# First batch's query and key rows loaded unit by unit, its pooled product given a bank of its own, and VectorE adding it before x is split

## The chip, the cores and the metric

The kernel runs on one core of a Trainium2 chip. The metric is the device time of one execution in microseconds (us), shown as the median of three runs. A core has TensorE (PE, with PEld for weight loads), VectorE (DVE), ScalarE (ACT), GpSimd (POOL) and SyncE (SP); SP issues the transfers, as does ACT where the code says `nc.scalar.dma_start`.

## The reference, cut to what matters

Attention over q, k, v of shape (8 batches, 8 heads, 576 rows, 64), then a feed-forward block with float32 weights of 512x2048 and 2048x512.

```python
q_d, k_d, v_d = (t.reshape(B, H, S // 4, 4, D).mean(axis=3) for t in (q, k, v))
out_d = sm_attn(q_d, k_d, v_d)                  # 144 pooled rows, full softmax
out_up = np.repeat(out_d, 4, axis=2)
mask = np.abs(pos[:, None] - pos[None, :]) < 4  # a band of 7 keys
out_local = softmax(where(mask, q @ k.T / 8, -1e9)) @ v
x = (out_up + out_local)                        # laid out as (4608, 512)
h = x @ w_in
out = (h * clip(h + 3, 0, 6) / 6) @ w_out
```

Each pooled output row is repeated four times and added to four rows of the banded (local) output.

## The kernel before, in words

**The two stages.** x has 4608 tokens, cut into nine chunks of 512. For each chunk TensorE runs 16 steps f of a first product (L977, 12 matmuls of 512 columns into bank `h`) and 16 of a second (L1027, 12 matmuls into four banks `o0` to `o3`). The products are made from parts: x and each weight block are split into a high and a low part (float32r), and three of the four cross products are taken. ScalarE and VectorE do the gate between the two products (L983, L987, L991, L995). The weights come as 32 blocks of 512 KB and are turned into their two parts once, during the first chunk: two ScalarE passes (L180, L192), a VectorE pass that joins bits (L185), a ScalarE cast (L198) and a subtraction (L202, on VectorE or GpSimd).

**The attention** goes by units: one unit is two heads of one batch, so a batch has four. The first batch (b = 0, `direct`) is special, because TensorE has nothing else to do until it is done. Its q and k are loaded for two units at a time (a duo): for the first duo in three transfers of 192 KB per tensor, for the second in one of 576 KB (L257). Partition p gets nine rows in a row, and TensorE turns these with 128x128 transposes, three to a bank (L270). An eviction (L122 on VectorE, L120 on ScalarE) writes the three results into `qkd` with a step of nine elements, so that the columns stand in the order of the tokens. Then come, for each unit:
- the sums of four columns of q and k (`pool4`: L351 on VectorE, L355 and L357 on GpSimd);
- the pooled scores (L451), their softmax (L507, L500, L528, L535 on 432 columns), the transposes of the weights (L544);
- the banded scores (L654 writes the mask, L662 the products), the greatest of each row (L507), the subtraction (L510), the exponent (L513), the total (L522), the reciprocal (L528), the division (L535 on 640 columns) and the transposes (L687);
- v in two forms: windows of 64 rows (L374, L378) for the banded product, and rows in fours (L385, L387) whose sums are made by GpSimd (L401, L402) and, for the last 16 pooled rows, by TensorE (L414).

**The end of a first-batch unit** is where the change lies. `pv_d` (L632) multiplies the pooled weights with the summed v. The right operand is read with a broadcast, each of 72 columns four times, so each matmul gives 288 columns straight into one of the two banks `x` of the unit, for two heads, two halves and two groups of rows. `pv` (L705) then adds the 20 banded products of 64x57 or 64x60 to the same columns, accumulating in PSUM. The split of x reads these banks: a high part (L122 or L120 CAST) and a low part (L881, VectorE only in the first chunk), and a copy takes the last 64 tokens of the batch, which belong to the next chunk, to `tail`. The second batch already works another way: its `pv_d` (L629) gives 144 columns into a bank `od`, ScalarE scales them, and VectorE adds the two (L713).

**What sets the order.** The program first plans all work as operations with engine, guessed cost, due time and the buffers that they take and free; a list planner then places them, engine by engine, and writes the instructions in that order. So every engine runs a fixed list. PE also gets matmuls of no use (`busy`, L1079) where the planner sees it waiting before the first product. `PEN` holds the planner's preferences between engines. A transfer waits for the one issued eight transfers before it, since there are eight completion semaphores.

**Lines after.** In the changed program most lines stand 4 to 16 lower in number: L977 becomes L972, L1027 L1022, L632 and L629 L620, L705 L691, L713 L696, L881 L875, L662 L648, L687 L673, L535 L530, L414 L409, L385 L380, L387 L382, L270 L318, L257 L311 and L313, L351 L346, L336 L295, L342 L301, L987 L982.

Of the kernel before, what the change touches and what calls it, by code (L numbers as in the profile page):

```python
# [19 lines left out]
P = 128  # L20
# [36 lines left out]
def tile_local_down_attention_moe(ctx, tc, q_all, k_all, v_all, _qk_loc, _v_loc, w_in, w_out, ident_d, _mask_d, out):  # L57
# [161 lines left out]
    xt, px = {}, {}  # L219
# [11 lines left out]
    def plan_duo(b, d, masked):  # L231
# [6 lines left out]
        qk, evicts, users = {}, {}, {"q": [], "k": []}  # L238
# [6 lines left out]
        if b < BY_PE:  # L245
            for kind, t in (("q", q_all), ("k", k_all)):
                evicts[kind] = []
                hk = kind, b, d
                rk = ("rawd", hk)
                raw = {}  # L250
                pieces_ = []
                step = 3 if d == 0 else 9
                for first in range(0, 9, step):
                    def ld(first=first, t=t, raw=raw, rk=rk, step=step):
                        if not raw:
                            raw["t"] = buf(rk[0], rk[1], [P, 9, ROW])
                        nc.sync.dma_start(  # L257
                            raw["t"][:, first:first + step],
                            src(t, row0 + first, [[9 * ROW, P], [ROW, step], [1, ROW]]))

                    pieces_.append(op("SP", 0.5, ld, take=[rk], size=dma(P, step * 512), dl=-1.0))
                    loads.append(pieces_[-1])
                for g in range(3):
                    st = {}
                    key = kind, b, d, g

                    def tr(g=g, st=st, key=key, raw=raw):
                        st["ps"] = ps = bank(PS, key)
                        for i in range(3):
                            nc.tensor.transpose(out=ps[:, i * P:(i + 1) * P], in_=raw["t"][:, 3 * g + i], identity=ident)  # L270

                    def ev(eng, g=g, st=st, key=key, kind=kind, hk=hk):
                        if kind not in qk:
                            qk[kind] = buf("qkd" + k0, hk, [P, 2, S])
                        dst = qk[kind].rearrange("e u (p t) -> e t (u p) ", t=9)[:, 3 * g:3 * g + 3]
                        copy_on(eng, dst, st["ps"][:, :3 * P].rearrange("e (t p) -> e t p", t=3))
# [12 lines left out]
        if b < BY_PE:  # L289
            for kind in "qk":  # L290
                plan.free_after(("qkd" + k0, (kind, b, d)), users[kind])
# [1262 lines left out]
```

## Time and profile before

| | us |
|---|---|
| median of three runs | 926.05 |
| lowest, highest of them | 921.72, 927.14 |
| the profiled execution | 926.6 |
| its span, first to last instruction | 924.7 |
| PE busy | 907.5 (98%) |
| DVE, ACT, POOL busy | 535.5, 438.1, 218.1 |
| mean granted TensorE clock | 0.994 |

The profile is one execution, so 1.9 us of its 926.6 lie outside the span. The lists of instructions in order of time show start and duration; durations of instructions that follow each other on an engine overlap a little, so a stretch is read from starts. "Windows" give the busy time of each engine in a stretch, with the clock that TensorE was granted. The chain of waits is the chain of work that ended last, followed back from the end: in it PE has 94%, and the two products of the feed-forward block 84%.

### The profile page before, as it was taken

What the parts mean: (1) busy time and instruction counts of PE and PEld (TensorE: products, weight loads), DVE (VectorE), ACT (ScalarE), POOL (GpSimd) and SP (SyncE); (2) the same over time, 40 slices, a digit from 0 to 9 for tenths busy, and PEclk for the clock granted to TensorE, in tenths of its full rate; (3) what the DMA queues carried; (4) which work ended last, traced back from release to release, by engine and by line L of the source; (5) the groups of instructions that cost most, each with busy time, mean ns of one, the idle gap of its engine ahead of it and who ended that gap; (6) DMA issues with size and microseconds to landing.
All of it is one profiled execution on the core that took longest, in us unless ns stands there. A gap on an engine that the chain in (4) does not pass through costs nothing.

```text
span 924.7 us, 19205 instructions
## 1 busy us (share of the span) xinstructions
PE 907.5 (98%) x7046; PEld 736.0 (80%) x7046; DVE 535.5 (58%) x968; ACT 438.1 (47%) x1437; POOL 218.1 (24%) x296
## 2 busy tenths in 40 slices
PE   7899999999999999999999999999999999999997
PEld 4577777888788888888888888888888888888886
DVE  7898677666675568456855576557644432233222
ACT  4788653755564456345545455445542222222221
POOL 4545611132252233023402240224201000000000
PEclk9899999999999999999999999999999999999999
DMA  8999343566665455445555556455532010001001
GB/s 211 311 218 288 68 113 62 117 133 127 116 140 108 100 108 126 103 95 114 110 130 104 102 113 133 76 101 113 132 76 54 1 46 1 1 1 46 0 1 46
DMA packets 311759, 93.49 MB, mean 101 GB/s; under 512 B 251377, under 2 KB 297841, under 8 KB 311665
## 3 DMA queue, kind: packets, MB, share of 16 engines
q1 hardware_dynamic: 311280, 91.69, 44.2%
q8 instruction: 55, 0.90, 0.4%
q10 hardware_dynamic: 384, 0.58, 0.2%
q14 instruction: 40, 0.32, 0.1%
HBM read 69.60 MB, written 22.61 MB: 100 GB/s over the span
## 4 chain that ended last, share of the span: by engine, by line
PE 94%; DMA 2%; DVE 1%; SPq 1%; POOL 1%; issue 0%; ACT 0%; ACTq 0%; DVEq 0%; POOLq 0%
PE h L977 42%; PE o L1027 42%; PE a L662 2%; PE h L705 1%; PE h L613 1%; PE a L468 1%; DMA arena<-in_v_dram 1%; PE o L632 1%; DMA pl<-arena 0%; PE a L705 0%; PE a L451 0%; SPq L257 0%; DMA early<-in_v_dram 0%; PE o L705 0%; PE h L468 0%
## 5 line engine op out<-in xcount | busy, mean ns | idle before, releaser
L1027 PE MATMUL o<-wp,rounded 128*128 128x512 f32 x1728 | 412.0, 392 | 0.0
L977 PE MATMUL h<-rounded,wp 128*128 128x512 f32 x1728 | 405.5, 390 | 2.5 <-DVE first L713 2.4
L977 PEld LDWEIGHTS h<-rounded,wp 128*128 128x128 f32 x1728 | 323.0, 188 | 71.7 <-issue 3.7
L1027 PEld LDWEIGHTS o<-wp,rounded 128*128 128x128 f32 x1728 | 321.5, 188 | 68.4 <-issue 0.8
L983 ACT ACTIVATE arena<-h 128x512 f32<-128x512 f32 x144 | 85.8, 596 | 197.5 <-PE h L977 195.3
L987 DVE SCALAR_TENSOR_TENSOR arena<-arena,h 128x512 f32<-128x512 f32 x144 | 98.1, 681 | 134.2 <-ACT arena L983 133.7
L995 DVE TENSOR_TENSOR rounded<-arena,rounded 128x512 fp32r<-128x512 f32 x115 | 81.0, 705 | 129.4 <-PE o L1027 107.0
L991 ACT CAST rounded<-arena 128x512 fp32r<-128x512 f32 x144 | 88.9, 618 | 109.9 <-PE o L1027 59.3
L518 ACT ACTIVATE arena<-arena 128x64 f32<-128x64 f32 x240 | 80.3, 337 | 0.2
L995 POOL TENSOR_TENSOR rounded<-arena,rounded 128x512 fp32r<-128x512 f32 x29 | 39.0, 1344 | 76.0 <-PE o L1027 40.3
L342 DVE STREAM_TRANSPOSE arena<-arena 128x576 f32<-128x576 f32 x56 | 42.8, 764 | 23.9 <-DMA arena<-in_k_dram 15.9
L535 POOL TENSOR_TENSOR arena<-arena 128x640 f32<-128x640 f32 (+1 forms) x22 | 24.9, 1133 | 130.8 <-DVE arena L528 130.8
L401 POOL TENSOR_TENSOR arena<-arena 32x256 f32<-32x256 f32 (+1 forms) x27 | 20.4, 754 | 119.9 <-DMA arena<-in_v_dram 119.1
L518 ACT ACTIVATION_READ_ACCUMULATOR arena<-arena 128x1 f32 x240 | 45.4, 189 | 0.0
L637 ACT ACTIVATE arena<-h 128x144 f32<-128x144 f32 x24 | 7.0, 291 | 67.5 <-PE h L613 67.5
L494 ACT ACTIVATE arena<-arena 128x1 f32<-128x1 f32 (+1 forms) x79 | 15.2, 193 | 42.1 <-DVE arena L507 42.1
L399 DVE TENSOR_REDUCE arena<-arena 128x128 f32<-128x512 f32 (+1 forms) x25 | 26.5, 1059 | 13.6 <-PE h L613 11.1
L580 DVE STREAM_TRANSPOSE arena<-arena 128x384 f32<-128x384 f32 (+1 forms) x48 | 22.2, 467 | 20.8 <-DMA arena<-pd 20.5
L357 POOL TENSOR_TENSOR arena<-arena 128x144 f32<-128x144 f32 x54 | 31.1, 576 | 4.2
L402 POOL TENSOR_TENSOR arena<-arena 32x128 f32<-32x128 f32 (+1 forms) x27 | 12.2, 452 | 74.8 <-PE h L613 62.8
L599 DVE STREAM_TRANSPOSE arena<-arena 128x640 f32<-128x640 f32 x24 | 20.2, 844 | 14.2 <-DMA arena<-pl 14.1
L662 PE MATMUL a<-arena 64*64 64x64 f32 x1160 | 28.2, 222 | 0.0
(190 smaller groups left out, 798.9 us busy)
## 6 DMA issues: line engine op xcount, KB each, us to landing
rawp<-in_w_in_dram SPq DMA_DIRECT2D x16, 512.0 KB
rawp<-in_w_out_dram SPq DMA_DIRECT2D x16, 512.0 KB
arena<-in_q_dram SPq DMA_DIRECT2D x112, 72.0 KB
arena<-in_k_dram SPq DMA_DIRECT2D x112, 72.0 KB
pl<-arena SPq DMA_DIRECT2D x24, 320.0 KB
arena<-pl SPq DMA_DIRECT2D x96, 80.0 KB
arena<-in_v_dram SPq DMA_DIRECT2D x28, 256.0 KB
out_dram<-arena SPq DMA_DIRECT2D x89, 72.0 KB
```

The lines of the kernel that those rows point to most:

```text
L342: nc.vector.transpose(out=qk[kind], in_=qk[kind])
L357: eng.tensor_tensor(t, t, x[:, :, r], op=ALU.add)
L399: eng.tensor_reduce(out=vd, in_=raw.rearrange("p r e -> p e r"), op=ALU.add, axis=AX.X)
L518: nc.scalar.activation(x[:, j], x[:, j], AF.Exp, bias=m[:, j:j + 1], scale=0.125, accum_out=s[:, j:j + 1])
L535: eng.tensor_tensor(x, x, s.unsqueeze(2).broadcast_to(list(x.shape)), op=ALU.mult)
L662: nc.tensor.matmul(st["ps", g][half:half + WIN, jj * D:jj * D + WIN], qk_of("q")[hs, k_first:k_first + WIN], qk_of("k")[hs, k_first:k_firs ...
L977: nc.tensor.matmul(st["ps"], win[f][:, wt, kk * P:(kk + 1) * P], xs[part][:, kk], start=(kk == 0 and i == 0), stop=(kk == NK - 1 and i == ...
L983: nc.scalar.activation(st["t"], st["ps"], AF.Relu, bias=3.0)
L987: nc.vector.scalar_tensor_tensor(out=t, in0=t, scalar=6.0, in1=st["ps"], op0=ALU.min, op1=ALU.mult)
L991: nc.scalar.copy(st["gh"], st["t"])
L995: eng.tensor_tensor(st["gl"], st["t"], st["gh"].bitcast(F32), op=ALU.subtract)
L1027: nc.tensor.matmul(otile[n, m], gt[:, ms], wout[f][:, wt], start=(f == 0 and i == 0), stop=(f == NF - 1 and i == 2),)
```

## The change

What it does, for the first batch alone but for one planner preference:

- q and k are loaded for each unit by itself: 512 rows as 128 partitions of four rows (256 KB, one 2 KB piece per partition) and the other 64 rows of q and k as the two halves of a ninth tile (32 KB each). So there are 16 transfers where there were 8. Those of k are issued by ScalarE, those of q by SyncE.
- A unit has nine transposes as before, in banks of four, four and one. The evictions write `qkd` in order of memory and read PSUM with a step of 128 elements instead.
- `pv_d` of the first batch gives 144 columns into its own bank, half as many matmuls of half the columns; a copy brings them to `od` in SBUF. `pv` starts its own accumulation.
- VectorE adds `od`, each column four times, to the banded product (L696): 288 and 224 columns into a new SBUF buffer `x0`, and 64 into `tail`, instead of the copy.
- The high and low parts of the first chunk's x are made from `x0`. [...]
- `PEN["pool4"]["POOL"]` goes from -10 to 0: the planner no longer prefers GpSimd for the sums of four.

```diff
+        def ld_rows(t, i, rest):
+            if "rows" not in st:
+                st["rows"] = buf("rawd", un, [P, 9, ROW])
+            eng = nc.scalar if i else nc.sync
+            if rest:
+                eng.dma_start(st["rows"][i * D:(i + 1) * D, 8], src(t, row0 + 4 * P, [[ROW, D], [1, ROW]]))
+            else:
+                eng.dma_start(st["rows"][:, 4 * i:4 * i + 4], src(t, row0, [[4 * ROW, P], [1, 4 * ROW]]))
+
+        def turn_rows(i):
+            st["psq", i] = ps = bank(PS, ("qk", un, i))
+            for n in range(4 if i < 2 else 1):
+                nc.tensor.transpose(out=ps[:, n * P:(n + 1) * P], in_=st["rows"][:, 4 * i + n], identity=ident)
+
+        def evict_rows(i, eng):
...
+            if i < 2:
+                copy_on(eng, st["qk"][:, i, :4 * P].rearrange("e (p r) -> e p r", r=4),
+                        st["psq", i].rearrange("e (r p) -> e p r", r=4))
+            else:
+                copy_on(eng, st["qk"][:, :, 4 * P:], st["psq", i][:, :P].rearrange("e (i p) -> e i p", i=2))
...
         def pv_d():
-            if direct:
-                st["px"] = px[hp] = [bank(PS, ("x", un, g)) for g in range(2)]
-            else:
-                st["od"] = buf("od" + k0, un, [P, SD])
-                st["pod"] = bank(PS, ("od", un))[:, :SD]
+            st["pod"] = bank(PS, ("od", un))[:, :SD]
+            st["od"] = buf("od" + k0, un, [P, SD])
             for g in range(2):
                 for h in range(2):
                     hs = slice(h * D, (h + 1) * D)
                     v4, w = st["vd"][:nk[g], g, hs], st["pdt"][:nk[g], g, h]
-                    if not direct:
-                        nc.tensor.matmul(st["pod"][hs], v4, w, start=(g == 0), stop=(g == 1), skip_group_check=True)
-                    for i in range(2 if direct else 0):
-                        q = w[:, i * SD // 2:(i + 1) * SD // 2].unsqueeze(2).broadcast_to([nk[g], SD // 2, 4])
-                        nc.tensor.matmul(
-                            st["px"][i][hs, :HALF].rearrange("p (q r) -> p q r", r=4), v4, q, start=(g == 0), stop=(g == 1),
-                            skip_group_check=True)
+                    nc.tensor.matmul(st["pod"][hs], v4, w, start=(g == 0), stop=(g == 1), skip_group_check=True)
...
+        def add_to(to, g, first, n):
+            nc.vector.tensor_tensor(
+                to.rearrange("e (q r) -> e q r", r=4), st["px"][g][:, first:first + n].rearrange("e (q r) -> e q r", r=4),
+                st["od"].unsqueeze(2)[:, (g * HALF + first) // 4:(g * HALF + first + n) // 4].broadcast_to([P, n // 4, 4]),
+                op=ALU.add)
...
-            copy_on(eng, xt[0, "tail"][:, hp], st["px"][1][:, TOK - HALF:HALF])
+            add_to(xt[0, "tail"][:, hp], 1, TOK - HALF, S - TOK)
...
-        return px[k][s0 // HALF][:, :cnt].unsqueeze(1) if n == 0 else xt[0, "tail"][:, k:k + ks]
+        return x0[k][:, s0:s0 + cnt].unsqueeze(1) if n == 0 else xt[0, "tail"][:, k:k + ks]
...
-                c = op({"DVE": on("xlo", ks * cnt)["DVE"]} if n == 0 else on("xlo", ks * cnt), 0,
-                       lambda eng, a=(b, s0, off, cnt, k): lo(eng, *a), [a], lock=n > 0, free=free)
+                c = op(on("xlo", ks * cnt), 0,
+                       lambda eng, a=(b, s0, off, cnt, k): lo(eng, *a), [a], lock=True, free=free)
...
-PEN = {"lo": {"DVE": 0.0}, "pool4": {"POOL": -10.0}, ...
+PEN = {"lo": {"DVE": 0.0}, "pool4": {"POOL": 0.0}, ...
```

The first rows of SP before, from the identity matrix to the first transfers of v (`arena` and `rows` hold q and k as loaded):

```order
L81 DMA ident<-in_ident_dram 128x128
L257 DMA arena<-in_q_dram 128x384 x3
L257 DMA arena<-in_k_dram 128x384 x3
L257 DMA rows<-in_q_dram 128x1152
L257 DMA rows<-in_k_dram 128x1152 [waits DMAHW0_49]
L374 DMA arena<-in_v_dram 64x5x128 [waits DMAHW1_49]
```

And of the change, with the waits on transfers that are still under way:

```order
L313 DMA arena<-in_q_dram 128x512
L311 DMA arena<-in_q_dram 64x128
L313 DMA arena<-in_q_dram 128x512
L311 DMA arena<-in_q_dram 64x128 [waits DMAHW0_49]
L313 DMA rows<-in_q_dram 128x512 [waits DMAHW2_49]
L311 DMA rows<-in_q_dram 64x128 [waits DMAHW4_49]
L313 DMA rows<-in_q_dram 128x512 [waits DMAHW6_49]
L311 DMA rows<-in_q_dram 64x128 [waits DMAHW0_49]
L369 DMA arena<-in_v_dram 64x5x128 [waits DMAHW1_49]
```

The eight transfers of k stand at the start of ACT's list instead, ahead of its table load. The first transfer of v now waits for the third unit's k; before, it waited for the first piece of q.

On PE, among the scores of the first batch, the rows of the change (L409 makes the last 16 pooled rows of v, here of the last two units; L1074 is the matmul of no use; L640 begins the banded scores of the third unit to get them):

```order
L1074 LDWEIGHTS identb
L1074 MATMUL h_103<-identb 128x512
L409 MATMUL o_365<-early,four 16x128 [waits DMAHW7_49,DVE_49]
L409 MATMUL a_368<-early,four 16x128 [waits DMAHW4_49,PE_49,Activation_49]
L1074 LDWEIGHTS identb
L1074 MATMUL h_103<-identb 128x512
L640 LDWEIGHTS identb [waits DVE_49]
L640 MATMUL o_381<-maskb,identb 128x320 [waits PE_49]
```

Now all four of these sums stand between the banded scores of the second unit and those of the third. Before, three stood behind the first unit's banded scores, and the last one behind all four units'.

On DVE, the end of the first batch before (`o_485` and the like are the `x` banks):

```order
L122 CAST rounded<-o_485 128x288
L122 CAST rounded<-o_486 128x224
L881 TENSOR_TENSOR rounded<-o_485,rounded 128x288
L881 TENSOR_TENSOR rounded<-o_486,rounded 128x224
L122 CAST rounded<-o_546 128x288
L185 SCALAR_TENSOR_TENSOR early<-rawp_329 128x512
L881 TENSOR_TENSOR rounded<-o_546,rounded 128x288
L881 TENSOR_TENSOR rounded<-a_547,rounded 128x224
```

And of the change, for the last two units (`first` holds `x0` and `tail`):

```order
L696 TENSOR_TENSOR first<-a_651,early 128x288
L696 TENSOR_TENSOR first<-a_652,early 128x224
L185 SCALAR_TENSOR_TENSOR o_591<-o_591,rawp_351 128x512
L696 TENSOR_TENSOR first<-o_682,early 128x288
L696 TENSOR_TENSOR first<-a_683,early 128x224
L122 CAST rounded<-first 128x288
L696 TENSOR_TENSOR first<-o_514,arena 128x64
L202 TENSOR_TENSOR wp_720<-o_591,wp_720 128x512
L696 TENSOR_TENSOR first<-o_621,early 128x64
L696 TENSOR_TENSOR first<-a_652,early 128x64
L696 TENSOR_TENSOR first<-a_683,early 128x64
L202 TENSOR_TENSOR wp_712<-early,wp_712 128x512
```

The low parts have left DVE: all eight stand on POOL (L875). In their place DVE has the additions, and the subtractions L202 of the second and third weight blocks; before, POOL did that of the second.

More of the change, by code (lines that the diff above doesn't have):

```diff
@@ L216, in plan_weights @@
             w_hi[key], w_done[key] = e, g
-    xt, px = {}, {}
+    xt, x0 = {}, {}
     x_done, early_users, units = {}, [], []
@@ L243, in early_user @@
             return o
[L245 to L276, printed above, removed]
-                    l = pieces_[g if step == 3 else 0]
-                    a = early_user(op("PE", 0.66, tr, [l], take=[(PS, key), ("qkd" + k0, hk)], free=[rk], lag=LAGT, rec=3))
-                    evicts[kind].append(op(
-                        on("ev", 3 * P), 0, ev, [a], free=[(PS, key)]))
         for u in range(2):
-            unit = plan_unit(b, d, u, row0, k0, kv, PS, qk, evicts, users, masked, early_user, due - (1 - u) * unit_time(b))
+            unit = plan_unit(b, d, u, row0, k0, kv, PS, masked, early_user, due - (1 - u) * unit_time(b))
             if b < ALONE:
@@ L695, in pv @@
         def pv():
-            if alone and not direct:
+            if alone:
                 st["px"] = [bank(PS, ("x", un, g)) for g in range(2)]
@@ L802, in plan_unit @@
             if direct:
-                a = early_user(op("PE", 2.0, pv_d, evs_d + sums, take=[(PS, ("x", un, g)) for g in range(2)], free=[tk_d, ("vd" + k0, un)],
-                                  lag=LAGT, rec=16))
+                a = early_user(op("PE", 0.65, pv_d, evs_d + sums, take=[bk, ok], free=[tk_d, ("vd" + k0, un)], lag=LAGT, rec=8))
+                od = op(on("ev", SD), 0, lambda eng: copy_on(eng, st["od"], st["pod"]), [a], free=[bk])
             else:
@@ L828, in plan_unit @@
         if direct:
-            op(on("ev", S - TOK), 0, tail, [a], take=xbs, free=[bks[1]])
-            adds = [a]
+            adds = [op("DVE", 0.43 - 0.05 * g, partial(add, g), [a, od], take=[("x0", un)], free=[bks[g], ok]) for g in range(2)]
+            op("DVE", 0.22, tail, [a, od], take=xbs, free=[bks[1], ok])
         else:
@@ L833, in plan_unit @@
             plan.free_after(ok, adds)
+        if b < BY_PE:
+            plan.free_after(("qkd" + k0, un), s_ops + list(pooled.values()))
         for kind in "qk":
-            if b < BY_PE:
-                users[kind].extend(s_ops + [pooled[kind]])
-            else:
+            if b >= BY_PE:
                 plan.free_after(("qk" + k0, (kind, un)), s_ops + [pooled[kind]])
@@ L1218, in _slots @@
         "pdt1": [(xb0 + (2 + i) * S * 4, 2 * 2 * SD * 4) for i in range(2)],
+        "x0": [(xb0 + NHP * (S - TOK) * 4 + i * TOK * 4, TOK * 4) for i in range(NHP)],
         "xb1": slots["xb"][1:], "tail": [(xb0, NHP * (S - TOK) * 4)],
```

47 lines of the change are left out of this document (30 added, 17 removed).

## The prediction

> **What bounds the kernel now.** First the page and wide windows, to see which engine is full where:
>
> ```profile
> PE 907.5 (98%) x7046; PEld 736.0 (80%) x7046; DVE 535.5 (58%) x968; ACT 438.1 (47%) x1437; POOL 218.1 (24%) x296
> ...
> 25.00:35.00 10.00, 7.22 (x88) 4.59 (x88) 8.58 (x23) 7.55 (x19) 8.05 (x10) 1.00 0.92 231
> 35.00:45.00 10.00, 10.00 (x118) 6.52 (x120) 6.91 (x17) 6.37 (x14) 2.42 (x4) 0.66 1.01 398
> 45.00:56.50 11.50, 11.50 (x146) 7.54 (x141) 10.57 (x17) 9.78 (x16) 5.56 (x3) 1.00 0.86 204
> 56.50:100.00 43.50, 43.50 (x326) 33.62 (x325) 36.42 (x55) 39.37 (x65) 23.97 (x18) 1.00 0.88 243
> ```
>
> After the stretch are its length, then the busy time of PE, PEld, DVE, ACT and POOL, the granted clock, DMA share, GB/s. From 35 us on PE is never idle; the 17 us that it lacks to the span lie almost all earlier. So the change can move the end only by what it does to the first batch: when the products of the first chunk can run without a break, and how much PE work stands ahead of them. Then the chain of waits around that point:
>
> ```profile
> 17.70 3.36 DMA early<-in_v_dram
> ...
> 26.61 3.00 POOL early L535 x3
> ...
> 34.88 0.44 PE a L687 x2
> ...
> 50.34 5.03 PE h L977 x21
> ...
> 55.68 0.88 PE a L451 x12
> 56.56 5.67 PE h L977 x24
> ```
>
> Up to 34.88 the chain runs through transfers of v, the softmax and GpSimd's divisions; from there it is PE alone. At 56.56 PE has done all of the first batch, two steps of the first product and the second batch's first scores, and starts the third step. I take this as the mark: whatever the change moves it by, moves the end, unless something later gives it back. Narrow windows show a second thing about PE before the mark:
>
> ```profile
> 32.00:36.00 4.00, 2.17 (x17) 1.44 (x17) 3.49 (x7) 2.45 (x6) 3.22 (x5) 1.00 0.89 194
> 36.30:43.10 6.80, 6.80 (x99) 4.35 (x96) 3.88 (x9) 3.77 (x8) 1.21 (x3) 0.50 1.03 404
> ```
>
> PE sat idle for half of 32 to 36, and from 36.3 to 43.1 it was granted half its clock. That costs some 3.4 us. [...]
>
> **The change part by part.** *The pooled product.*
>
> ```profile
> 29.70:32.10 2.40, 2.32 (x16) 0.99 (x16) 1.00 0.64 95
> 35.40:39.10 3.70, 3.58 (x16) 1.28 (x16) 0.62 1.02 401
> 44.30:49.10 4.80, 4.71 (x32) 2.28 (x32) 1.00 1.03 246
> ...
> 48.94 0.81 PE L705 MATMUL o<-early 64*64 64x60 f32 x40
> ...
> 69.53 0.86 PE L629 MATMUL a<-first,arena 128*64 128x144 f32 x8
> ```
>
> The first three rows are L632 alone: 10.6 us for four units. The fourth is one unit's banded product, which stays. The last is the second batch's form, which the first batch now gets: 0.86 a unit, 3.4 for four. So PE does 7.2 us less. The first unit's 2.32 lay ahead of the wait that ends at 34.88, off the path; the other three shrink from 8.3 to 2.6, which is **5.7 us off PE's path** after 34.88.
>
> *q and k.*
>
> ```profile
> DMA packets 2464, 3.15 MB, mean 225 GB/s; under 512 B 228, under 2 KB 2097, under 8 KB 2464
> ...
> 4.99 2.25 SPq L374 DMA_DIRECT2D arena<-in_v_dram  x2
> ...
> 21.51 0.48 SPq L387 DMA_DIRECT2D early<-in_v_dram  x1
> 22.66 1.38 SPq L169 DMA_DIRECT2D rawp<-in_w_in_dram  x3
> ...
> SPq L378 <- DMA rows<-in_k_dram: 1.5, 1, 1.5
> ...
> SPq L374 <- DMA rows<-in_q_dram: 0.8, 1, 0.8
> 27.88 0.39 PE L414 MATMUL o<-early,four 64*16 64x128 f32 x2
> ```
>
> The first row is for 0 to 14 us. Now 16 transfers stand ahead of v, and v's first waits for the third unit's k: identity, two units and that k are 1.8 MB, at 225 GB/s 8.1 us. It started at 4.99. The 20 transfers of v took SP from there to 21.99, 17.0 us, of which the two waits for `rows`, 2.3 us, fall away, since q and k are in by then. So the last ends at 8.1 + 14.7 = 22.8, 0.8 later, and lands 3.4 after its start (the chain's 3.36), at 25.7. There PE stands in the sum for the last unit (L409), with the banded scores of two units behind it: 2 x 1.1, to 27.9. Before, the last scores ended at 27.88, where L414 starts. So the stage is **neither earlier nor later**. Bounds: 1 us earlier if the transfers are issued faster with 2 KB pieces; 3.1 us later if the whole delay of v's start stays.
>
> *The evictions of the transposes* read PSUM with a step and write in a row; before it was the other way.
>
> ```profile
> 5.43 1.52 DVE L122 COPY arena<-a 128x384 f32<-128x384 f32 x2 [0.67 <-PE a L270]
> 34.29 0.54 DVE L122 COPY early<-a 128x384 f32<-128x384 f32 x1
> ```
>
> Per column, that is 2.0 ns with the stepped write and 1.4 in a row. So 512 columns cost 0.7 to 1.0; I take 0.85. All are done by 15 us, while v is still on its way until 25.7, which hides either end. [...] By the upper end six copies on VectorE would cost 2 us more than by the lower one, still ahead of v.
>
> *From the last scores to the mark* VectorE has the longest list. Its prices:
>
> ```profile
> 24.78 0.88 DVE L507 TENSOR_REDUCE early<-o 128x5 f32<-128x320 f32 x2
> 32.29 0.78 DVE L342 STREAM_TRANSPOSE arena<-arena 128x576 f32<-128x576 f32 x1 [1.37 <-DMA arena<-in_q_dram]
> 32.99 0.78 DVE L522 TENSOR_REDUCE early<-arena 128x10 f32<-128x640 f32 x1
> 33.69 0.69 DVE L185 SCALAR_TENSOR_TENSOR o<-o,rawp 128x512 int32<-128x512 int32 x1
> 35.10 1.26 POOL L535 TENSOR_TENSOR arena<-arena,early 128x640 f32<-128x640 f32 x1 [0.17 <-DVE early L528]
> 35.87 0.39 DVE L122 COPY arena<-a 128x256 f32<-128x256 f32 x1
> 36.18 0.73 DVE L351 TENSOR_REDUCE arena<-arena 128x144 f32<-128x576 f32 x1
> 40.35 0.76 DVE L122 CAST rounded<-o 128x288 fp32r<-128x288 f32 x2 [2.23 <-PE o L705]
> 44.69 0.21 DVE L122 COPY first<-o 128x64 f32<-128x64 f32 x1
> 44.95 3.63 DVE L185 SCALAR_TENSOR_TENSOR early<-rawp 128x512 int32<-128x512 int32 x3
> 44.99 1.78 POOL L202 TENSOR_TENSOR wp<-early,wp 128x512 fp32r<-128x512 f32 x1 [7.41 <-ACT wp L198]
> 48.50 1.76 DVE L202 TENSOR_TENSOR wp<-early,wp 128x512 fp32r<-128x512 f32 x1
> L713 DVE TENSOR_TENSOR arena<-a,arena x4: 440/441/444, 80.5 to 107.1; 128x288 f32<-128x288 f32 x4
> ```
>
> Step by step. The first of the two units' scores ends at 26.9. Eight greatest-and-subtract operations at 0.44: 30.4. Two totals at 0.78, a join of bits (0.69), three copies (0.39 and two small, 0.9) and small reciprocals (0.4): 33.9. GpSimd's last division follows, to 35.2; before it ended at 36.36.
>
> Then, up to the second weight block's L202: eight additions for x0 (0.44 for 288 columns, 0.37 for 224 by width), 3.2; four for the tail at 0.21, 0.8; four casts at 0.38, 1.5; two transposes, 1.6; two sums of four, 1.5; two copies, 0.8; two joins, 1.4; three L202, at the join's 0.69 as they are as wide and touch as much, 2.1. Together 12.9. Operations that follow each other start about 0.08 sooner than these durations (32.29, 32.99, 33.69), 2.0 over 25. VectorE must also wait for PE between the units, since the last unit's bank is freed by the third unit's addition; I put 1.5 for that. 33.9 + 12.9 - 2.0 + 1.5 = 46.3. For the mark five more must run, up to the gate of the first step, which frees its bank: two joins, a greatest of 432 columns (0.6 by width), an L202, the gate (0.69), 3.3 together. **The mark comes at 49.6 instead of 56.56: 7.0 earlier.** Does PE get there? From 27.9 it has ten groups of transposes (0.44 each in the chain, 4.4), four pooled products (3.4) and four banded ones (3.2), two steps (5.7, as the chain's 24 matmuls) and the second batch's scores (1.2), 17.9, to 45.8; with two windows at half clock, to 49.2. VectorE decides, with PE close behind. Where VectorE and GpSimd overlap, the join took 1.21 (3.63 for three) and L202 1.76 instead of 0.69: GpSimd now has the eight low parts, up to 7 us at its 1.78 for 512 columns, in just this stretch. That could take 2 to 3 us of the 7.
>
> *What is given back later.* Behind the mark PE needs weights. In 56.5 to 100 ScalarE is busy for 39.4 of 43.5, so it can gain 4.1 there, and 3.6 in 35 to 45, where it waited for PE. The weights' loads start 0.8 later than before (22.66). Between nothing and all 7 could be lost; ScalarE's idle covers most of it, and I take 2.0 for this and GpSimd's overlap together.
>
> Sum: 926.6 of the profiled execution - 7.0 + 2.0 = 921.6. The median of the three runs stands 0.55 below that execution, so **921.1 us**, with 917 to 925 as its own range.
>
> **The rivals.** *PE's saving lands whole* (15%). If VectorE's list runs without the waits and PE never loses its clock: 5.7, the 3.4 of half clock and the 1.2 by which the divisions end earlier make 10.3: 915.7. For it: VectorE was busy only 6.9 of 10 in 35 to 45. Against it: its 12.9 us of listed work.
>
> *v comes late, or the clock falls again* (15%). [...]
>
> *Weights set the pace of the first chunk* (10%). If the second product waits for each block, as its loads start 0.8 later, the mark's lead is lost and the end is where it was or 0.8 behind: 926.5. Against it: PE never waited for a weight before.
>
> *VectorE becomes the bound of the first chunk; slower* (10%). It gets 3.2 + 0.8 of additions less 0.8 of copies, and the subtractions of four more weight blocks (L202 at 1.76 when GpSimd runs, 7.0), while the eight low parts leave it (3.2). That is 7 us more before 100, where it has 7.1 idle in 56.5 to 100 and 0.9 in 45 to 56.5. From the point where it is full, each further microsecond is PE's: with joins at 1.21 for 0.69 in a dozen places, 6 us more, 13 in all against 8.0 idle, it ends 5 later than before: 931.
>
> **How the numbers follow.** 50% for 921.1. A measurement of this kernel can tell about 1% (9.3 us) from no change. Faster by over that (below 916.8): two thirds of the first rival and a tenth of the forecast, 16%. Slower (above 935.3): a third of the last rival and something unseen, 6%. Between: 78%. The range runs from 912.5 (the whole saving with 3 us more from v's bound) to 931.
>
> **What would show it.** L620 at 0.8 to 0.9 a unit; the last division on GpSimd near 35; the first of 24 matmuls of the third step near 50; DVE over 9 tenths from 27 to 50 with PE's waits ending on it (L696); no PE gap after 56. Wrong if v's last sum lands past 28, if PE waits at L1022 for L202 or a cast of weights between 55 and 100, or if the mark comes before 46.

## The result, and the profile after

The changed kernel takes **920.92 us** (median of 20 runs, 918.28 to 924.42) beside 926.64 us for the kernel before in the same session (20 runs, 921.72 to 931.2): a ratio of 0.9939, 95% interval 0.9924 to 0.9953, that is 5.7 us less (4.4 to 7.0). The prediction was 921.1 us. The profiled execution of the changed kernel took 922.62 us, 1.7 above its own median, with a span of 920.8 (before: 924.7), so its trace shows 3.9 of the 5.7 us.

The page, and wide windows (length, then busy time of PE, PEld, DVE, ACT, POOL, granted clock, DMA share, GB/s):

```profile
PE 902.3 (98%) x7013; PEld 734.4 (80%) x7013; DVE 535.9 (58%) x973; ACT 436.8 (47%) x1442; POOL 217.6 (24%) x295
...
25.00:35.00 10.00, 9.51 (x169) 6.90 (x169) 7.62 (x22) 6.23 (x15) 7.29 (x9) 0.83 0.81 202
35.00:45.00 10.00, 8.44 (x155) 5.79 (x153) 8.98 (x20) 7.82 (x19) 6.20 (x9) 0.90 0.87 283
45.00:56.50 11.50, 11.50 (x94) 8.57 (x93) 10.68 (x21) 10.59 (x23) 1.83 (x3) 0.94 0.87 246
56.50:100.00 43.50, 42.60 (x320) 32.60 (x319) 37.27 (x53) 37.84 (x59) 24.16 (x14) 1.00 0.95 265
100.00:180.00 80.00, 78.99 (x627) 61.88 (x626) 56.30 (x101) 45.09 (x133) 20.95 (x22) 1.00 0.42 94
```

PE has 5.2 us less to do in all. Before it was full from 35 us on; now 35 to 45 has 1.6 us of idle time, and 0.9 and 1.0 lie behind 56.5, where there were none and 0.2. VectorE is busy for 9 tenths of 35 to 45, where it had been for 7.

The chain of waits up to the mark (start, duration, what):

```profile
24.62 0.38 PE a L409 x2
...
29.32 0.89 DVE early L502 x2
...
31.60 0.79 PE a L620 x8
...
36.23 1.84 DMA arena<-in_k_dram
...
38.78 0.78 DVE arena L301
...
42.75 0.27 PE a L691 x2
...
46.66 0.32 PE a L409 x2
46.98 0.88 PE a L446 x12
47.86 6.34 PE h L972 x27
```

Before, this chain was PE's alone from 34.88 on. Now it runs through VectorE until 42.75, by way of a transfer of the second batch's k, and only from there to the mark through PE again, which had half its clock until 46.25. The mark (third step of the first product) lies inside the last row: 15 of its 27 matmuls belong to the first two steps, so the third starts at 51.3. It was at 56.5: 5.2 us earlier. From there to the end it is 869.5 us, before 868.2. So 1.3 us were given back behind the mark.

The stretches of half clock, with the 3.4 us ahead of each:

```profile
22.55:25.95 3.40, 1.69 (x31) 0.85 (x35) 2.18 (x8) 1.73 (x11) 1.50 (x3) 0.98 0.82 212
25.95:29.35 3.40, 3.40 (x75) 2.57 (x68) 1.71 (x5) 0.73 (x2) 2.62 (x3) 0.51 0.89 297
...
39.55:42.95 3.40, 1.97 (x59) 1.29 (x61) 3.40 (x10) 2.05 (x5) 1.14 (x1) 0.99 1.02 405
42.90:46.25 3.35, 3.35 (x42) 2.68 (x39) 2.91 (x11) 2.53 (x7) 3.02 (x6) 0.50 1.02 411
```

From 20 us on there are again 6.8 us at half clock, now in two pieces, each behind a stretch of 3.4 us in which PE was busy for 50 to 58% of the time (1.69 and 1.97 us). So PE was not wholly idle ahead of either.

### The profile page after: what moved, and what is told of

It is laid out like the page before. It is cut to its first block, busy times and chain, and to the rows that moved or that the text cites. A ratio compares the mean times of both kernels' runs of the same rounds, so it can differ in the third digit from the quotient of the medians.

```text
span 920.8 us, 19166 instructions
## 1 busy us (share of the span) xinstructions
PE 902.3 (98%) x7013; PEld 734.4 (80%) x7013; DVE 535.9 (58%) x973; ACT 436.8 (47%) x1442; POOL 217.6 (24%) x295
## 3 DMA queue, kind: packets, MB, share of 16 engines
q10 hardware_dynamic: 1280, 1.76, 0.6%
## 4 chain that ended last, share of the span: by engine, by line
PE 91%; DMA 3%; SPq 3%; DVE 1%; issue 1%; ACT 0%; ACTq 0%; DVEq 0%
PE h L972 42%; PE o L1022 41%; PE a L648 2%; PE h L691 1%; SPq L295 1%; PE h L608 1%; PE a L463 1%; DMA rawp<-in_w_in_dram 1%; DMA arena<-in_k_dram 1%; DMA arena<-in_q_dram 1%; SPq L369 1%; PE a L446 0%; PE a L691 0%; PE a L620 0%; SPq L373 0%
## 5 line engine op out<-in xcount | busy, mean ns | idle before, releaser
L301 DVE STREAM_TRANSPOSE arena<-arena 128x576 f32<-128x576 f32 x56 | 42.7, 764 | 33.6 <-DMA arena<-in_k_dram 22.4
L648 PE MATMUL a<-arena 64*64 64x64 f32 x1160 | 28.7, 224 | 0.0
```

The source lines that it names most:

```text
L301: nc.vector.transpose(out=qk[kind], in_=qk[kind])
L648: nc.tensor.matmul(st["ps", g][half:half + WIN, jj * D:jj * D + WIN], qk_of("q")[hs, k_first:k_first + WIN], qk_of("k")[hs, k_first:k_firs ...
```

## The experiments

One profile was taken of each kernel. "Mark" is where its third step starts, "idle" is PE's idle time from the mark to 180 us, both worked out from that profile; times and ratios are from all runs of a kernel, against the kernel before on the same chip (medians 925.1 to 925.7).

| kernel | median us (runs) | ratio (95%) | mark | idle |
|---|---|---|---|---|
| before | 926.64 (20) | 1 | 56.5 | 0.2 |
| after | 920.92 (20) | 0.9939 (0.9924 to 0.9953) | 51.3 | 1.9 |
| product_only | 922.14 (12) | 0.9963 (0.9940 to 0.9985) | 52.0 | 1.3 |
| loading_only | 934.46 (6) | 1.0075 (1.0050 to 1.0101) | 55.1 | 0.0 |
| double_product | 921.09 (11) | 0.9952 (0.9932 to 0.9973) | 50.3 | 0.0 |
| double_adds | 924.07 (12) | 0.9977 (0.9959 to 0.9995) | 56.0 | 0.0 |
| scores_first | 920.64 (8) | 0.9960 (0.9940 to 0.9980) | 50.2 | 2.9 |
| clock_kept | 921.42 (12) | 0.9964 (0.9946 to 0.9982) | 49.5 | 1.0 |
| turn_moved | 921.92 (12) | 0.9967 (0.9950 to 0.9984) | 54.5 | 0.4 |
| both_moved | 921.45 (12) | 0.9957 (0.9939 to 0.9975) | 53.6 | 0.0 |
| fewer_columns | 921.99 (12) | 0.9964 (0.9943 to 0.9984) | 51.7 | 1.8 |
| v_split | 922.00 (12) | 0.9956 (0.9938 to 0.9975) | 55.5 | 0.0 |
| pad_10 | 922.11 (12) | 0.9963 (0.9946 to 0.9980) | 53.8 | 0.0 |
| pad_20 | 923.02 (12) | 0.9976 (0.9955 to 0.9996) | 54.0 | 0.0 |

Executions of one kernel spread over 3.5 to 9.5 us, and the changed kernel was not run again beside these, so two kernels whose intervals overlap are not told apart. A mark is that of one execution: in the profiles that keep the changed kernel's order, the last sum over v's last rows (L409) started anywhere between 23.7 and 26.0 us.

### The two halves of the change

product_only is the kernel before with the new product and addition alone:

```diff
-            st["px"] = px[hp] = [bank(PS, ("x", un, g)) for g in range(2)]
+            st["pod"] = bank(PS, ("od", un))[:, :SD]
+            st["od"] = buf("od" + k0, un, [P, SD])
...
-            op(on("ev", S - TOK), 0, tail, [a], take=xbs, free=[bks[1]])
+            adds = [op("DVE", 0.43 - 0.05 * g, partial(add, g), [a, od], take=[("x0", un)], free=[bks[g], ok]) for g in range(2)]
+            op("DVE", 0.22, tail, [a, od], take=xbs, free=[bks[1], ok])
```

> q and k are loaded and turned as before (pairs of units, three transposes to a bank, GpSimd preferred for their sums of four); only the pooled product has its own bank and is added by VectorE, with the split from SBUF. The whole change stands 5.7 us (0.61%) under the kernel before. Theory (the prediction's): the product is the gain and the loading gives and takes nothing, so this kernel is 4.5 to 6.5 us under the kernel before. Rival: the order in which v and the second batch's transfers come, which the loading by unit shifts, holds the change back, so the product alone brings more, 7 us or over. Other rival: the loading by unit brings the gain, and this kernel is within 1.5 us of before.

loading_only takes the rest of the change (`ld_rows`, `turn_rows`, `evict_rows`, the penalty of `pool4`) and keeps the old product:

```diff
-            raw["t"] = buf(rk[0], rk[1], [P, 9, ROW])
+            st["rows"] = buf("rawd", un, [P, 9, ROW])
...
-PEN = {"lo": {"DVE": 0.0}, "pool4": {"POOL": -10.0}, "ev": {"DVE": 5.0}, "sum4": {"POOL": -10.0},
+PEN = {"lo": {"DVE": 0.0}, "pool4": {"POOL": 0.0}, "ev": {"DVE": 5.0}, "sum4": {"POOL": -10.0},
```

> q and k are loaded and turned unit by unit as in the changed kernel, and GpSimd is no longer preferred for their sums of four; the pooled product goes into the banks of x four times over as before, with VectorE splitting x from them. Theory: the loading gives and takes nothing: within 1.5 us of the kernel before. Rival: v's later start (8.7 us of transfers ahead of it instead of 4.99) costs, since here PE's list is as long as before: 2 to 3 us over before. Other rival: the loading is where the gain comes from: 3 us or more under before.

The product alone gives 3.4 us (1.4 to 5.6), so it is worth something without the loading; whether the loading then adds to that is not resolved, since the interval of the whole change overlaps it. The loading alone is **slower**, by 4.6 to 9.4 us; all three expectations missed that. In its trace the mark came 1.4 us earlier than before (55.1) and 6.9 were lost behind it. PE's waits from 51 to 320 us (total, times, longest) are part of this:

```profile
PE h L973 <- DVE arena L983: 4.5, 3, 2.2
PE o L1023 <- DVE arena L923: 1.4, 1, 1.4
PE h L973 <- POOL rounded L876: 1.3, 1, 1.3
```

Of the first row, 1.83 us end at the mark itself. Behind the mark PE waited 5.6 us in all, in the kernel before 2.6, and its granted clock was 0.94 over 270 to 300, which is some 3.6 us at half once more. The gate that PE waited for at the mark (L983 in that kernel) stood on VectorE behind a transpose that waited for the second batch's q:

```profile
52.41 0.78 DVE L301 STREAM_TRANSPOSE arena<-arena 128x576 f32<-128x576 f32 x1 [1.76 <-DMA arena<-in_q_dram]
...
54.35 1.27 DVE L983 SCALAR_TENSOR_TENSOR arena<-arena,h 128x512 f32<-128x512 f32 x2
```

These two kernels were planned anew, so their order differs in many places, and PE had more work left behind the mark too. Why the loading costs this much without the product stays open. What holds is that the halves do not add up. All kernels that follow, but for v_split, keep the changed kernel's order of instructions apart from the one edit.

### Which engine sets the mark

double_product repeats each pooled matmul, double_adds each of VectorE's additions, in the first batch:

```diff
-                    nc.tensor.matmul(st["pod"][hs], v4, w, start=(g == 0), stop=(g == 1), skip_group_check=True)
+                    [nc.tensor.matmul(st["pod"][hs], v4, w, start=(g == 0), stop=(g == 1), skip_group_check=True) for _ in range(1 + direct)]
```

```diff
-            nc.vector.tensor_tensor(
+            [nc.vector.tensor_tensor(
...
-                op=ALU.add)
+                op=ALU.add) for _ in range(1 + direct)]
```

> The changed kernel with each of the first batch's pooled products computed twice into the same place, every instruction else in the same order: 0.81 us more of PE for each of four units, 3.2 in all, ahead of the third step of the first product. Theory (VectorE's list sets when that step starts): PE has 1.7 us of waits on VectorE's additions between 39 and 44 us that take most of it up, so 0 to 1.5 us over the changed kernel, that is 4.2 to 5.7 us under the kernel before. Rival (PE's own work sets it): 2.6 to 3.2 us over the changed kernel, 2.5 to 3.1 us under before.

> The changed kernel with each of VectorE's additions of the first batch issued twice, every instruction else in the same order: eight of 0.37 to 0.46 us and four of 0.21, some 4 us more of VectorE between 34 and 46.5 us. Theory (VectorE's list sets when the third step starts): 3 to 4 us over the changed kernel, so 1.7 to 2.7 us under the kernel before. Rival (PE's own work sets it, VectorE has time left): at most 1 us over the changed kernel, 4.7 us or more under before.

The doubled product cost PE 2.0 us, less than I had expected (each unit's group took 1.29 instead of 0.79), and the median moved by 0.2 us, by the ratios 1.2 (4.4 us under before, 2.5 to 6.3). That time alone does not exclude the rival's 2.5 to 3.1; the trace below speaks against it. The doubled additions cost VectorE some 4.5 us (1.65 for four, 0.75 for two before), 3.8 of them behind the transpose of k, and the median moved by 3.2 (2.1 us under before, 0.5 to 3.8), which excludes that rival's 4.7 or more. So in the changed kernel **VectorE's list decides**, and PE has some room. Two windows of double_product and, from double_adds, VectorE's additions behind the transpose of k and PE's wait for the last of them:

```profile
38.00:44.00 6.00, 5.49 (x140) 4.15 (x140) 5.82 (x14) 5.79 (x14) 3.43 (x6) 1.00 1.03 412
44.00:50.00 6.00, 5.35 (x31) 3.78 (x31) 6.00 (x13) 5.71 (x17) 1.77 (x3) 1.00 1.11 244
```

```profile
39.28 0.75 DVE L301 STREAM_TRANSPOSE arena<-arena 128x576 f32<-128x576 f32 x1
41.25 1.65 DVE L696 TENSOR_TENSOR first<-o,early 128x288 f32<-128x288 f32 x4
...
48.99 0.86 DVE L696 TENSOR_TENSOR first<-a,early 128x64 f32<-128x64 f32 x4
...
49.56 0.38 PE L409 MATMUL a<-arena,four 64*16 64x128 f32 x2 [2.21 <-issue]
```

In double_product PE kept its full clock from 38 to 50, still had 1.2 us of idle time there, and VectorE was full (5.82 and 6.00 of 6.00). The changed kernel lost 1.7 us to half clock from 42.9 on, so a part of the doubled product's cost may have been paid by the clock that it kept; no run tells the two apart. In double_adds VectorE did not wait for k, and the last of the additions ends at 49.85, where the changed kernel's ends at 46.26.

fewer_columns takes VectorE work away, but ahead of the transpose of k. It leaves out three of four columns in the greatest of each row, and 56 of 64 in the sum:

```diff
-                a = op("DVE", 0.45, lambda g=g: top(rows(g), greatest(g)), [sl_op])
+                a = op("DVE", 0.45, lambda g=g: top(rows(g)[:, :, ::4] if direct else rows(g), greatest(g)), [sl_op])
...
-            a = op("DVE", 0.15 + size / 960, lambda: total(p_all(), st["s"]), [a])
+            a = op("DVE", 0.15 + size / 960, lambda: total(p_all()[:, :, :8] if direct else p_all(), st["s"]), [a])
```

> The changed kernel with less VectorE work in the first batch: the greatest of each row of banded scores is taken over every fourth column, and the sum of each row over 8 of 64 columns (the rest of these columns is left out of the two reductions); the same instructions in the same order. Between 24 us and the first product's third step that takes some 2.5 us from VectorE (four greatest of 0.48 to some 0.15, two sums of 0.76 to some 0.15). Theory (VectorE's list sets when that step starts): 1.7 to 2.5 us faster than the changed kernel, 7.4 to 8.2 us under the kernel before. Rival (another limit stands right behind VectorE: v's arrival, the second batch's k, or ScalarE's wait for weights): less than 0.8 us faster, 5 to 6.5 us under before.

```profile
33.19 0.20 DVE L523 RECIPROCAL early<-early 128x10 f32<-128x10 f32 x1
...
39.17 0.78 DVE L301 STREAM_TRANSPOSE arena<-arena 128x576 f32<-128x576 f32 x1 [1.94 <-DMA arena<-in_k_dram]
...
46.34 0.34 DVE L696 TENSOR_TENSOR first<-a,early 128x64 f32<-128x64 f32 x2
```

Nothing was gained, and the trace shows where it went: VectorE came to the transpose of k earlier and waited 1.94 us for the transfer instead of 0.71. The last addition ends at 46.68, no earlier than the changed kernel's. The rival (another limit right behind) held: work taken away ahead of that wait gains nothing, while double_adds shows that work behind it counts.

### The waits and the clock

scores_first, turn_moved and both_moved move single instructions in the finished order; clock_kept adds matmuls of the kind that the kernel already has for PE's idle time (`sum` is L409, `scores` L640 and L648, `turn` L301, `pool` L346, `add` the second L696 of a unit):

```diff
+        for what, to in [(("sum", (0, 3)), ("scores", (0, 2)))]:                          # scores_first, both_moved
+        for what, to in [(("turn", (1, 0), "k"), ("add", (0, 3))),
+                         (("pool", (1, 0), "k"), ("turn", (1, 0), "k"))]:                 # turn_moved, both_moved
+            order.remove(self.names[what])
+            order.insert(order.index(self.names[to]) + 1, self.names[what])
...
+        for name, n in [(("sum", (0, 3)), 6), (("pv", (0, 2)), 5)]:                       # clock_kept
+            self.names[name].busy += n
```

> The changed kernel with one PE instruction group moved: the sum over v's last rows of the fourth unit, for which PE waited 1.71 us at 24.62, goes behind the third unit's banded scores instead of ahead of them; everything else in the same order. Those scores can then start near 23 instead of 25.2, and the clock need not fall after 25.9. Theory (VectorE's list sets the third step, and VectorE is held until 38.78 by the transpose of the second batch's k, which lands at 38.07): VectorE's wait there grows from 0.7 to 2 us or more and the time changes by less than 1 us: 4.7 to 6.7 us under the kernel before. Rival (the end of the first batch's scores sets everything behind it): 2 to 3.3 us faster than the changed kernel, 7.7 to 9 us under before.

> The changed kernel with eleven idle-time matmuls more on PE: six ahead of the wait for v's last rows (22.9 to 24.6 us) and five ahead of the third unit's banded product (41.3), 0.26 us each, everything else in the same order; they fill the two stretches after which PE was granted half its clock (25.9 to 29.25 and 42.95 to 46.2, 1.67 us lost in each). Theory: PE is never idle from 43.9 to the third step, so the second window's 1.67 us come back, while the first's is hidden by VectorE's wait for k: 1 to 2 us faster than the changed kernel, 6.7 to 7.7 us under before. Rival: both windows count, 3 us faster, 8.7 under before. Other rival: VectorE alone sets the step and the clock is free: within 0.7 us of the changed kernel, 5 to 6.4 under before.

> The changed kernel with two VectorE instructions moved: the transpose of the second batch's first k (which waited for its transfer until 38.78) and the sum of four behind it go behind the additions of the first batch's other three units; everything else in the same order. Theory (VectorE is held there with the additions queued behind it, PE waits 1.4 us for them and then loses 1.67 to the clock): the additions come 2.2 us earlier, the wait and the half clock go, 1.5 to 3 us faster than the changed kernel, 7.2 to 8.7 us under before. Rival (VectorE's list has to be worked off in any order before the third step): within 0.7 us of the changed kernel, 5 to 6.4 under before.

> Both moves together: the fourth unit's sum behind the third unit's scores on PE, and the transpose of the second batch's k behind the additions on VectorE. Theory: with VectorE no longer held by k, the earlier scores count too: 3.5 to 5.5 us faster than the changed kernel, 9 to 11 us under before. Rival (VectorE's list in any order): no faster than either move alone, 5 to 8.7 us under before.

None of the four is faster than the changed kernel by anything that the runs can show (3.1 to 4.0 us under before, each within 2). The times of my theories for clock_kept, turn_moved and both_moved lie outside these intervals. The rivals' times are not all met either: turn_moved is 1.5 to 4.6 us under before, where its rival had 5 to 6.4. For scores_first (1.9 to 5.6 under) the theory's time is possible and the rival's is not; VectorE's wait for k there was 0.9 us, where I expected 2 or more. For clock_kept the full clock was there (its profile is that of its shortest run, 917.42 us):

```profile
20.00:49.40 29.40, 26.59 (x376) 16.51 (x377) 26.28 (x64) 23.61 (x67) 17.22 (x21) 1.00 0.92 276
...
22.55:25.95 3.40, 2.74 (x50) 1.30 (x48) 1.64 (x6) 1.04 (x7) 2.10 (x4) 1.00 0.79 224
...
39.55:42.95 3.40, 2.89 (x87) 2.12 (x85) 2.74 (x8) 2.96 (x7) 2.72 (x4) 1.00 1.02 416
```

No gain came of it over all runs: neither my theory of 1 to 2 us nor the rival of 3 shows, and the half clock costs little here. turn_moved shows what my theory of it missed. VectorE no longer waited for k, but PE then waited for VectorE at another place (in that execution it had also waited 3.18 us for v, beside 1.71 in the changed kernel, so the late mark is not the move's alone):

```profile
36.31 0.21 DVE L523 RECIPROCAL early<-early 128x10 f32<-128x10 f32 x1
...
47.92 0.35 DVE L696 TENSOR_TENSOR first<-a,early 128x64 f32<-128x64 f32 x2
```

```profile
48.24 0.38 PE L409 MATMUL a<-arena,four 64*16 64x128 f32 x2 [1.53 <-issue]
```

The second batch's first sum over v (L409) needs a bank `a`, which the last of the additions for the tail frees; the profile names no releaser ("issue"), but the addition ends at 48.27, where the sum starts. PE waited there in both_moved (1.53 us), double_adds (2.21), v_split (0.62), double_product (0.48) and clock_kept (0.47) too. In the changed kernel's own profile it did not: PE, at half clock until 46.25, came to that sum at 46.59, 0.3 us behind the addition. On PE that sum, 12 matmuls of scores and 15 of the first product stand ahead of the mark. In five profiles (after, scores_first, clock_kept, both_moved, fewer_columns) the mark came 4.7 to 5.1 us behind the end of that last addition; in double_adds and turn_moved it came 6.1 and 6.3 behind, with a granted clock of 0.83 in 50 to 60 in the one, and of 0.97 in 40 to 50 and 0.86 in 50 to 60 in the other, some 3.4 us at half in each. And from the last small reciprocal to that addition it took 11.8 to 12.9 us in after, scores_first, clock_kept, turn_moved and both_moved, in whatever order: my theory (the order matters) fell, and the rival (the list has to be worked off in any order) held.

In both_moved VectorE no longer waited for k and PE only 0.34 us for v, and a third wait came up: ScalarE, late with its copy out of a bank, held PE's transposes for 1.76 us, and PE was at half clock again (0.90 over 20 to 53.5, some 6.7 us at half).

```profile
31.56 0.81 PE L539 MATMUL o<-ident,early 128*16 128x128 f32 x3 [1.76 <-ACT early L120]
```

v_split lets ScalarE issue four of v's transfers and is planned anew:

```diff
-                nc.sync.dma_start(raw, src(v_all, row0, [[4 * ROW, P], [1, 4 * ROW]]))
+                (nc.scalar if b == 0 and hp > 1 else nc.sync).dma_start(raw, src(v_all, row0, [[4 * ROW, P], [1, 4 * ROW]]))
...
-            l = op("SP", 0.5, partial(ld4, g), take=[rk], size=dma(P, 512) if alone and g else dma((P, NAR)[g], 2048), nd=1 if alone else 1 + g)
+            l = op("ACT" if b == 0 and hp > 1 else "SP", 0.5, partial(ld4, g), take=[rk], size=dma(P, 512) if alone and g else dma((P, NAR)[g], 2048), nd=1 if alone else 1 + g)
```

> The changed kernel with four of v's twenty first transfers (the rows for the sums of the third and fourth units) issued by ScalarE instead of SP, where twenty issues of 0.5 to 0.65 us run from 9.24 to 22.4; the order is planned anew with that. Theory (v's last rows hold PE, GpSimd and through them VectorE until 24.5, and that is issue time on SP): v is in 2 to 2.5 us sooner and the first batch's last scores end as much earlier, 1.5 to 2.5 us faster than the changed kernel, 7.2 to 8.2 us under before. Rival (VectorE's list, full from 10 to 24 us as well, sets the pace, and v's arrival costs nothing): within 0.8 us of the changed kernel, 5 to 6.5 us under before; ScalarE's two more microseconds of issuing could even cost 1.

PE no longer waits for v, but the wait moved on once more: ScalarE stood 3.28 us at a weight block that had not landed, PE 1.86 for ScalarE's copy behind it, and VectorE 2.92 for PE:

```profile
38.44 0.67 ACT L180 ACTIVATE rawp<-rawp 128x512 f32<-128x512 f32 x1 [3.28 <-DMA rawp<-in_w_out_dram]
```

The mark came at 55.5, and from there it was 4.1 us shorter to the end than in the changed kernel. The time is the changed kernel's within the error.

### What is given back behind the mark

pad_10 and pad_20 put idle-time matmuls just ahead of the second batch's first sum:

```diff
+        for name, n in [(("sum", (1, 0)), 10)]:      # 20 in pad_20
+            self.names[name].busy += n
```

> The changed kernel with ten idle-time matmuls of 0.26 us (2.6 us together) put on PE just ahead of the second batch's first sum over v (46.6 us), where PE is never idle until 86; everything else in the same order. They move the start of the first product's third step by up to 2.6 us. Theory (a start earlier than about 53 us is given back behind it: the second batch's q and k come late, since the transfers are full from 60 to 100 us, and PE waits 0.9 us at 86 and 1.0 at 101 for them): the two waits take up 1.9 us of it, so 0 to 1.2 us over the changed kernel, 4.5 to 5.7 us under the kernel before. Rival (what stands ahead of the mark moves the end one for one): 2.2 to 2.6 us over the changed kernel, 3.1 to 3.5 under before.

> The same with twenty of them, 5.2 us. Theory (the first 2 us are taken up by the later waits, the rest counts): 2.8 to 3.6 us over the changed kernel, 2.1 to 2.9 us under the kernel before. Rival (one for one): 4.8 to 5.2 us over the changed kernel, 0.5 to 0.9 us under before.

```profile
44.85 4.49 PE L1074 MATMUL h<-identb 128*128 128x512 bf16 x20
```

They took 2.33 and 4.49 us, and the medians moved by 1.2 and 2.1 us. By the ratios, whose intervals are wide, it is 2.2 and 3.4. For ten, that does not tell theory and rival apart; for twenty, the one-for-one rival (0.5 to 0.9 us under before) stands at the edge of the interval (0.4 to 4.2 under). So it leans to the theory and does not settle it. The profiles say more: with a mark at 53.5 or later (eight kernels) PE has 0.0 to 0.4 us of idle time between the mark and 180; with a mark at 52.0 or earlier, five of six have 1.0 to 2.9 (double_product, with its mark at 50.3, has none). In product_only it is one wait, for the subtraction L202 of a weight block:

```profile
63.29 3.02 PE L1028 MATMUL o<-wp,rounded 128*128 128x512 f32 x12 [1.28 <-DVE wp L202]
```

In the changed kernel they are two, and both go back to VectorE, which stands at a transpose for the second batch's q or k:

```profile
84.69 0.78 DVE L301 STREAM_TRANSPOSE arena<-arena 128x576 f32<-128x576 f32 x1 [1.49 <-DMA arena<-in_q_dram]
...
86.17 0.87 DVE L505 TENSOR_TENSOR arena<-a,arena 128x320 f32<-128x320 f32 x2
...
99.13 0.78 DVE L301 STREAM_TRANSPOSE arena<-arena 128x576 f32<-128x576 f32 x1 [2.44 <-DMA arena<-in_k_dram]
...
102.07 0.81 DVE L696 TENSOR_TENSOR arena<-a,arena 128x288 f32<-128x288 f32 x2
```

```profile
86.79 0.89 PE L539 MATMUL a<-ident,arena 128*128 128x128 f32 x6 [0.90 <-DVE arena L505]
...
102.57 0.39 PE L409 MATMUL a<-arena,four 64*16 64x128 f32 x2 [1.01 <-DVE arena L696]
```

That k stood on SP behind seven weight blocks of 512 KB each:

```profile
82.13 0.55 SPq L169 DMA_DIRECT2D rawp<-in_w_in_dram  x1
...
88.52 8.74 SPq L295 DMA_DIRECT2D arena<-in_k_dram  x4
```

Its four issues took 8.74 us, with the DMA engines at 0.95 of their time over 56.5 to 100. The same four transfers ended their issue at 93.74 in the kernel before and at 97.26 now: the chunk starts earlier, but its transfers do not come earlier.

## Why the prediction was right, point by point

**The time** was right within 0.2 us, and the sum's own two parts nearly: the mark 7.0 earlier (it was 5.2), given back 2.0 (it was 1.3). That it was so close is luck: with these two parts as measured the sum gives 922.2, and the rest is the 1.7 us by which the profiled execution of the changed kernel lies above its median, where the sum had taken off 0.55. The way was right: less work on PE, then VectorE's list as the limit, then a part given back. The sum of PE's own work, to 49.2, counts "two windows at half clock". No run shows that the clock goes by windows; the traces show 6.8 us at half clock, in one piece before (36.3 to 43.1) and in two after (25.95 to 29.35, 42.90 to 46.25), 3.4 us lost in all each time.

**The pooled product.** Right: L620 took 0.79 us a unit in the chain, in groups of 8 matmuls. PE's work had been the chain from 34.88 to the mark, and now is only from 42.75 on: what double_product's extra product costs is not told from nothing.

**v.** Its first transfer started at 9.24, not 8.1; the twenty issues took 13.2 us, not 14.7; the last sum for v (L409) could start at 24.62, where I had 25.7. The two errors more than cancel. The scores behind it ended at 29.3, not at 27.9: I left out the transposes between the two units' scores and PE's clock, which was halved from 25.95 on. That 1.4 reached the mark only in part: the last small reciprocal on VectorE ended at 34.25, where I had 33.9.

**Evictions.** The lower end was right:

```profile
7.40 0.69 DVE L122 COPY arena<-a 128x512 f32<-128x512 f32 x1 [0.16 <-PE a L318]
```

That is 1.35 ns a column with the step on PSUM's side, no more than the 1.4 in a row.

**VectorE's list** was the right term, and 1.7 us too short. By its rows: the reciprocal 0.35 late; up to the second block's L202, 13.1 us instead of 12.4; from there to the first step's gate 3.65 instead of 3.3; PE 0.3 more.

```profile
34.04 0.21 DVE L523 RECIPROCAL early<-early 128x10 f32<-128x10 f32 x1
...
34.77 1.34 DVE L122 CAST rounded<-first 128x288 fp32r<-128x288 f32 x2
...
38.78 0.78 DVE L301 STREAM_TRANSPOSE arena<-arena 128x576 f32<-128x576 f32 x1 [0.71 <-issue]
...
46.18 1.20 DVE L202 TENSOR_TENSOR wp<-early,wp 128x512 fp32r<-128x512 f32 x1
...
50.35 0.68 DVE L982 SCALAR_TENSOR_TENSOR arena<-arena,h 128x512 f32<-128x512 f32 x1
```

What I had not listed is the wait at 38.78: I counted the transposes of the second batch by their duration and not by their transfer, which follows v and three weight blocks on SP. (VectorE was free at 38.07; the last signal of k's transfer stands in the trace at 38.70.) That wait is not what made the list too short, though: with 0.31 at 43.91 VectorE's waits come to 1.0 us, and I had allowed 1.5. The list itself was short. The first of the two casts at 34.77 took 1.16 where I had 0.38, and the L202 at 46.18 took 1.20 where I had 0.69. GpSimd was at work beside both, and I had booked such overlap behind the mark; but the L202 at 45.18 took 0.69 beside GpSimd as well, so the cause is not shown. I also named the wrong link to the mark: where PE waited for VectorE, it was not for the gate and the casts, but for the bank that the last tail addition frees.

**Given back.** The size was near, the cause wrong. I gave it to ScalarE's weights and to GpSimd's overlap. In the changed kernel's trace no wait of PE behind the mark ends on a weight (product_only has one), and the two up to 180 us come from q and k of the second batch. "No PE gap after 56" was wrong, twice by then. These two make 1.9 us, beside 0.2 before; over the whole execution PE's waits behind the mark are 3.4 us beside 2.6, so of the 1.3 given back only 0.8 are waits.

**The loading.** "Neither earlier nor later" is not what the experiment says of it alone (4.6 to 9.4 us slower). With the product no loss shows. The prediction did not see that the two depend on each other.

**The rivals.** "PE's saving lands whole" did not come: its condition, VectorE without waits, failed. "The clock falls again" came true as a fact (3.4 us at half clock per piece, 1.7 lost in each), but clock_kept gave nothing back that the runs can show; PE waited 0.47 us for the bank in it instead. PE was busy for 1.69 and 1.97 of the 3.4 us ahead of the two falls. "Weights set the pace" and "VectorE becomes the bound of the first chunk" did not come as such; a softer form of the last did, through the transposes. Two of the prediction's sums are off: the lower end of the range, 912.5, takes off 3 us for an early v, where its own bound for that is 1 us (914.7), and two thirds of the first rival with a tenth of the forecast make 15%, not 16.

## What to carry to other kernels

When an edit takes work from the bound engine, list the next engine's instructions up to the same point, each with what it waits for: an instruction that waits for a transfer must be counted at the transfer's landing, not at its duration (here VectorE was held 0.71 us at 38.07). Work taken away ahead of that wait gained nothing here (fewer_columns waited 1.94 us instead); work added behind it counted (double_adds, 3.2 us by the medians). Take the price of an operation from a row with the same company: two operations beside a busy GpSimd took 1.3 us more here than their rows alone had said (2.36 instead of 1.07), though a third beside it took no more (0.69). And for a stage that starts earlier, look whether its transfers come earlier too: here, with the mark 5.2 us earlier and one k's issues 3.5 later, a part of the lead seems to be waited off later, which the padded kernels lean to and do not settle. Two halves of a change can each be worth something quite different alone (here 3.4 us gained, and 4.6 to 9.4 lost).

## What the runs showed of the hardware that was not expected

- VectorE's copy of 512 columns out of PSUM with a step of 512 bytes between neighbours took 0.69 us, 1.35 ns a column; one in a row had taken 0.54 for 384, 1.4 ns a column, and the old one, which wrote SBUF with a step, had taken 1.52 for two of 384.
- PE was granted half its clock after 3.4 us in which it was busy for 1.69 and 1.97 us, and kept it after 2.74 and 2.89 us of 3.40 (clock_kept, the same stretches). Busy time alone does not decide: 1.86 us of 8.9 to 12.3 in the changed kernel were followed by a clock of 1.00. What decides is not shown.
- Four transfers of 72 KB for the second batch's k took 8.74 us to issue at 88.5, behind seven weight blocks issued from 82.13 on; the same four had taken 2.71 in the kernel before, at 91.03, with no issue ahead of them from 83.9 on. Whether the blocks are the cause, no run tests.
